# Seven natural tiles in 64x64 bursts, split loads and a new order in front of the steady phases

## The chip, the cores and the metric

The kernel runs on one core of a Trainium2 chip. TensorE (PE) multiplies, with its weight loads (PEld) beside it; VectorE (DVE), ScalarE (ACT) and GpSimd (POOL) work on tiles; POOL also issues the loads, SyncE (SP) the stores and the transposes by DMA. The metric is the device time of one execution in microseconds (us), the median of several.

## The reference, cut to what matters

```python
# q, k, v: (4, 8, 768, 64) float32
gamma = 1.0 - 2.0 ** (-5.0 - np.arange(H))
for t in range(S):
    state = gamma * state + k[t] v[t]^T            # per batch and head, 64 x 64
    y[:, :, t] = 1 / sqrt(64) * q[t] state
x = y.transpose(0, 2, 1, 3).reshape(3072, 512)
h = x @ w_in                                       # 512 x 2048
s = np.sin(alpha * h)
g = h + s * s / (alpha + 1e-09)
out = g @ w_out                                    # 2048 x 512
```

## The kernel before

**Tiles.** A tile is 128 positions of one batch with all 8 heads: 24 tiles, six to a batch (c = 0 to 5). `order` takes the four first tiles of the batches, e0 to e3, and then the others, batch by batch; `P` is the same list, so P[4] is the fifth tile, and P[4] to P[8] are batch 0, P[9] to P[13] batch 1. `groups` (L53) are e0 to e3 as group 0, and then pairs: P[4] and P[5] are group 1, P[6] and P[7] group 2, and so on.

**Attention of a tile.** q and k are transposed (qkT), on PE (`half_T`, `stage_T`) or by DMA from SP (`turn`, L258). The scores within the tile go to PSUM (tile pa), are masked by DVE into aT, and multiply v, which has been scaled by a decay (`scale_v`, L143; mostly on POOL). The running state adds what earlier tiles left. DVE multiplies the sum by a decay table qg into xT, the transposed input of the feed-forward. The state is carried on: in PSUM (ps) with a block-diagonal bf16 copy (s_bd) written by ACT for natural tiles, and in float32 (s_f, added up by DVE) with a bf16 copy (s_q, written by ACT, by POOL in the last batch) for wide ones.

**Natural and wide tiles.** A natural tile is loaded with 128 positions on the 128 partitions (`load_chunk`); its matmuls use half of PE's rows or half of its columns (`stage_A`, `stage_M`, `stage_S`, `keep_S`). A wide tile (`wide(j)`, j >= 8 and not a first tile: P[10] and after) is loaded by `load_seq`, one DMA to a head for a whole batch, with half of the heads on each half of the partitions; its matmuls use quarters of the array, 64 by 64, and come in one `burst`: `inter` (state times q) of the old tile, `scores` of the new one, `sums` (k times v), then a `nop` that waits until `inter` is through, and `mix` (scores times v). A burst hands back what is run later: `mask` and `exit` (py to xT), `keep` (to s_f) and `hand` (s_f to s_q).

**Feed-forward.** A `Slot` makes 128 or more rows of h for a group: matmuls with w_in into ph (L450), sin on ACT (L453), its square on ACT or DVE (L458, L460), and the last step into gT on DVE (`add`, L465). `ff_out` multiplies gT by w_out into po (L475), 16 matmuls to an output tile; `take` copies po out of PSUM and stores it. `fill(n)` and `F(ts, fs)` place such output pieces by hand.

**PSUM.** Eight banks: four of tag mm (ph, po, transposes), two as the pair pa, and one each of tags ps and ty (py of the bursts, ps, py of the natural tiles, and for a while the first two output tiles).

**Order.** The schedule is by hand: each engine runs its instructions as the program emits them. The front works on e0 to e2 with idle matmuls between. Group 0 runs 128 columns short at first (slots 0 to 3 for three tiles, then one 4-slot strip for e3), then slots 4 to 15 with output pieces between. Lines 668 to 719 are the seam to group 1: the last pieces of group 0, transposes, attention of P[4] and P[5], and 16 `fill` pieces between. From then on `phase(g, ...)` runs each group in eight double slots, with the output pieces of the group before it between and the attention of two later tiles at slots 1 and 5 (2 and 5 in phase 1), by `at` and `where`.

**Queues.** POOL issues all loads of q, k, v and the weights in program order, with `scale_v` and the decay tables between; w_in and w_out come in four pieces each. SP issues the transposes by DMA and the stores, in program order.

Of the kernel before, what the change touches and what calls it, by code (L numbers as in the profile page):

```python
# [16 lines left out]
def kernel(  # L17
# [15 lines left out]
    nc = tc.nc  # L33
# [35 lines left out]

    def chunk_of(t, j):  # L70
# [19 lines left out]
    def spot(h):  # L90

        return h // NP, (h % NP) ^ (h // NP)

    def load_seq(bt, names="qkv"):
# [3 lines left out]
        if "q" in names:  # L98
# [3 lines left out]
        for name, src in (("q", q), ("k", k), ("v", v)):  # L102
            if name not in names:
                continue
            for h in range(H):
                b, at = spot(h)
                r = slice(64 * b, 64 * b + 64)
                o = tv[r, :, at, :] if name == "v" else tqk[r, :, "qk".index(name), at, :]
                nc.gpsimd.dma_start(out=o, in_=src[bt, h, cs[0] * C:, :].rearrange("(f i) d -> i f d", i=64))  # L109
# [8 lines left out]
    def load_w_in(i):  # L118
        nc.gpsimd.dma_start(out=w_in[:, :, i * fw:(i + 1) * fw], in_=w_in_v[:, :, i * fw:(i + 1) * fw])

    def load_w_out(i):
        nc.gpsimd.dma_start(out=w_out[:, i * fo:(i + 1) * fo, :], in_=w_out_v[:, i * fo:(i + 1) * fo, :])
# [25 lines left out]
    load_w_in(0)  # L148
# [5 lines left out]
    load_w_out(0)  # L154
# [38 lines left out]
    def later_tables():  # L193
        for b in range(2):
            for p in range(NP):
                nc.vector.memset(lgq[64 * b:64 * b + 64, p:p + 1], lng[NP * b + (p ^ b)])
# [23 lines left out]
    s_bd = [big.tile([128, NP, 128], BF16, name=f"s_bd{i}") for i in range(2)]  # L220
# [9 lines left out]
    def half_T(j, i, eng, tag="mm"):  # L230
# [3 lines left out]
        pt = psum.tile([128, NP, 128], BF16, name="pt", tag=tag, bufs=4 if tag == "mm" else 1)  # L234
# [8 lines left out]
    def stage_T(j, eng=None, tag="ty"):  # L243
        pt = psum.tile([128, 2 * NP, 128], BF16, name="pt", tag=tag, bufs=4 if tag == "mm" else 1)
        st["qkT", j] = work.tile([128, 2 * NP, 128], BF16, name="qkT", tag="qkT", bufs=6)
        for i in range(2):
            for p in range(NP):
                nc.tensor.transpose(pt[:, i * NP + p, :],
                                    raw["qk"[i], j][:, 2 * p:2 * p + 2, :].rearrange("p h d -> p (h d)"), ident)
# [24 lines left out]
    def stage_S(j):  # L274
        c = j % NCH
        if c == 0:
            st["ps"] = psum.tile([128, NP, D], F32, name="ps", tag="ps")
        ps = st["ps"]
        for p in range(NP):
            for e in range(2):  # L280
                nc.tensor.matmul(ps[64 * e:64 * e + 64, p, :], raw["k", j][:, 2 * p + e, :], raw["v", j][:, 2 * p + e, :],
                                 start=(c == 0 and p == 0), stop=True, skip_group_check=True)
        return ps

    def turned(to, ps, copy):

        copy(to[:, 0:2], ps[:, 0:2])
        for e in range(2):
            copy(to[64 * e:64 * e + 64, 2:4], ps[64 - 64 * e:128 - 64 * e, 2:4])

    def keep_S(j, ps):
        if wide(j + 1):
            turned(s_q[(j % NCH + 1) % 2], ps, nc.scalar.copy)
            return
        for e in range(2):
            r = slice(64 * e, 64 * e + 64)
            nc.scalar.copy(s_bd[(j % NCH + 1) % 2][r, :, r], ps[r, :, :])

    def stage_M(j, tag="ty"):
        c = j % NCH  # L300
# [3 lines left out]
        qkT, aT, vs = st["qkT", j], st["aT", j], raw["v", j]  # L304
        py = psum.tile([128, NP, 128], F32, name="py", tag=tag)
        if c > 0:
            for p in range(NP):
                for e in range(2):
                    r = slice(64 * e, 64 * e + 64)
                    nc.tensor.matmul(py[r, p, :], s_bd[c % 2][:, p, r], qkT[:, p, :],  # L310
                                     start=(p == 0), stop=True, skip_group_check=True)
        for p in range(NP):
            for e in range(2):
                nc.tensor.matmul(py[64 * e:64 * e + 64, p, :], vs[:, 2 * p + e, :], aT[:, e, p, :],
                                 start=(c == 0 and p == 0), stop=True, skip_group_check=True)
        x = xT[g][:, :, i * C:(i + 1) * C]
        if c == 0:
            nc.scalar.copy(x, py)
            return
        ps = stage_S(j) if c < NCH - 1 else None  # L320
        nc.vector.tensor_mul(x, py, qg[:, c])
        if ps is not None:
            keep_S(j, ps)
# [3 lines left out]
    def half(x):  # L327
        return slice(64 * x, 64 * x + 64)

    tiles4 = [(b, e) for b in range(2) for e in range(2)]  # L330

    def inter(j):

        qkT, s = st["qkT", j], s_q[j % NCH % 2]
        st["py", j] = [psum.tile([128, 512], F32, name=f"py{b}", tag=tag) for b, tag in enumerate(("ps", "ty"))]
        for m in range(2):
            for b, e in tiles4:
                last = nc.tensor.matmul(st["py", j][b][half(e ^ b), m * 128:(m + 1) * 128].rearrange("p (f i) -> p f i", f=2),  # L338
# [452 lines left out]
```

## Time and profile before

| what | us |
|---|---|
| median of 3 runs | 214.45 (213.43 to 217.16) |
| the profiled execution | 214.06 |
| its span, first to last instruction | 212.3 |
| PE busy | 203.6 |
| ACT busy | 158.7 |
| DVE busy | 153.3 |
| POOL busy, DMA issues included | 113.4 |
| first slot of group 0 starts | 15.94 |
| slot 4 starts | 24.18 |
| phase 1 starts | 49.99 |
| phase 2 starts | 62.52 |
| phase 3 starts | 78.99 |

The profiled execution is 1.8 us longer than its span. A busy PE is not PE at its peak. In the lists of waits a line gives who waited for whom, the total, how often and the longest; in the timeline, the start, the length, the engine, the line and the operation; in the table by stretch, the length and each engine's busy time in it. A line number is one of the kernel above.

### The profile page before, as it was taken

To read this page: it belongs to the slowest core of one execution; us is meant where nothing else is said; L and a number is where in the kernel's file an instruction comes from. 1 tells how busy PE (TensorE), PEld (TensorE's weight loads), DVE (VectorE), ACT (ScalarE), POOL (GpSimd) and SP (SyncE) were. 2 spreads that over 40 slices of the span, in tenths; PEclk is the share of its full clock that TensorE was granted. 3 is DMA by queue.
4 is the path that set the end of the run, shared out by engine and by line. 5 is a ranking of instruction groups with operands and counts; after the bars stand their busy time and mean duration, and the time that the engine had idled before them with its cause. 6 is when DMAs were issued, how large, how long until landed. Compare 5 with 4: busy or idle time off the path is not lost.

```text
span 212.3 us, 5584 instructions
## 1 busy us (share of the span) xinstructions
PE 203.6 (96%) x2242; PEld 131.0 (62%) x2242; DVE 153.3 (72%) x342; ACT 158.7 (75%) x335; POOL 113.4 (53%) x149
## 2 busy tenths in 40 slices
PE   7868989999999999999999999999999999999994
PEld 3534534457776766766666666667666666666653
DVE  5785599766887688688678787786887778666550
ACT  7677576877998887877867877876877777788821
POOL 8999877899889169899699821001121120000000
PEclk9999999999999999999999999999999999999999
DMA  9999999999999979999999994403713110110112
GB/s 131 149 172 197 206 206 175 138 194 184 136 149 83 211 78 155 173 91 156 155 163 133 164 146 102 99 12 90 78 39 88 56 45 7 49 49 3 49 49 99
DMA packets 100281, 24.74 MB, mean 117 GB/s; under 512 B 92816, under 2 KB 97312, under 8 KB 100256
## 3 DMA queue, kind: packets, MB, share of 16 engines
q0 software_dynamic: 77504, 13.38, 87.1%
q1 hardware_dynamic: 22608, 10.96, 26.0%
q8 instruction: 17, 0.28, 0.6%
q14 instruction: 8, 0.07, 0.1%
q10 hardware_dynamic: 144, 0.07, 0.1%
HBM read 27.27 MB, written 6.29 MB: 158 GB/s over the span
## 4 chain that ended last, share of the span: by engine, by line
PE 78%; DVE 7%; POOL 5%; DMA 4%; ACT 3%; issue 1%; DVEq 0%; POOLq 0%
PE po L475 36%; PE ph L450 34%; DMA w_out<-in_moe_w_out_dram 4%; DVE gT L465 4%; POOL qkr L84 2%; PE poh L500 2%; PE py L338 2%; DVE s L460 2%; ACT s L453 2%; PE py L381 1%; POOL vr L84 1%; DVE aT L271 1%; ACT s L458 1%; PE pa L349 1%; PE py L310 1%
## 5 line engine op out<-in xcount | busy, mean ns | idle before, releaser
L465 DVE SCALAR_TENSOR_TENSOR gT<-s,rec_alpha,ph 128x256 bf16<-128x256 f32 (+3 forms) x180 | 81.6, 495 | 34.1 <-ACT s L458 33.7
L453 ACT ACTIVATE s<-ph,alpha_sb 128x256 f32<-128x256 f32 (+3 forms) x180 | 78.5, 484 | 36.5 <-PE ph L450 36.4
L450 PE MATMUL ph<-xT,w_in 128*128 128x256 bf16 (+3 forms) x720 | 99.1, 280 | 2.4 <-DVE gT L465 1.2
L475 PE MATMUL po<-w_out,gT 128*128 128x512 bf16 x368 | 96.2, 380 | 0.8 <-DMA w_out<-in_moe_w_out_dram 0.7
L450 PEld LDWEIGHTS <-w_in 128*128 128x128 bf16 x720 | 69.7, 98 | 33.8 <-issue 2.6
L458 ACT ACTIVATE s<-s 128x512 f32<-128x512 f32 (+1 forms) x91 | 56.9, 625 | 2.9
L475 PEld LDWEIGHTS <-gT 128*128 128x128 bf16 x368 | 34.0, 98 | 27.2 <-DVE gT L465 1.8
L421 POOL CAST s_q<-s_f 128x256 bf16<-128x256 f32 x5 | 2.0, 396 | 44.3 <-DVE s_f L415 25.7
L143 POOL TENSOR_TENSOR v_seq<-v_seq,kgq 128x512 bf16<-128x512 bf16 x14 | 14.6, 1066 | 11.4 <-issue 6.4
L109 POOL DMA_DIRECT2D qk_seq<-in_q_dram x24 | 17.1, 755 | 2.4 <-DMA v_seq<-in_v_dram 2.2
L109 POOL DMA_DIRECT2D qk_seq<-in_k_dram x24 | 17.0, 738 | 1.7 <-DMA qk_seq<-in_q_dram 1.6
L109 POOL DMA_DIRECT2D v_seq<-in_v_dram x24 | 17.0, 743 | 0.8 <-DMA qk_seq<-in_k_dram 0.6
L487 DVE COPY o_sb<-po 128x512 f32<-128x512 f32 x19 | 13.1, 691 | 5.2 <-PE po L475 5.2
L358 DVE TENSOR_TENSOR aTw<-pa,maskq 128x768 bf16<-128x768 f32 x14 | 13.3, 951 | 0.0
L408 DVE TENSOR_TENSOR xT<-py,qg 128x256 bf16<-128x256 f32 x28 | 10.5, 415 | 0.0
L519 PE MATMUL spare<-warm 128*128 128x512 bf16 x25 | 9.1, 492 | 1.2 <-DVE warm L161 1.2
L143 POOL TENSOR_TENSOR vr<-vr,kg 128x512 bf16<-128x512 bf16 x9 | 9.5, 1056 | 1.0 <-DMA vr<-in_v_dram 0.8
L84 POOL DMA_DIRECT2D vr<-in_v_dram x10 | 9.3, 931 | 1.1 <-DMA w_out<-in_moe_w_out_dram 0.5
L271 DVE TENSOR_TENSOR aT<-pa,mask 128x1024 bf16<-128x1024 f32 x6 | 7.3, 1219 | 2.3 <-PE pa L267 2.3
L84 POOL DMA_DIRECT2D qkr<-in_q_dram x9 | 8.3, 923 | 1.1 <-DMA w_out<-in_moe_w_out_dram 0.6
L84 POOL DMA_DIRECT2D qkr<-in_k_dram x9 | 8.2, 909 | 1.0 <-DMA w_out<-in_moe_w_out_dram 0.5
L460 DVE TENSOR_TENSOR s<-s 128x512 f32<-128x512 f32 x6 | 6.5, 1080 | 2.6 <-ACT s L453 2.6
(94 smaller groups left out, 145.9 us busy)
## 6 DMA issues: line engine op xcount, KB each, us to landing
out_dram<-o_sb SPq DMA_DIRECT2D x23, 256.0 KB, 3.4
w_in<-in_moe_w_in_dram POOLq DMA_DIRECT2D x4, 512.0 KB, 13.0
w_out<-in_moe_w_out_dram POOLq DMA_DIRECT2D x4, 512.0 KB, 14.0
vr<-in_v_dram POOLq DMA_DIRECT2D x10, 128.0 KB, 6.1
qk_seq<-in_q_dram POOLq DMA_DIRECT2D x16, 80.0 KB, 6.7
qk_seq<-in_k_dram POOLq DMA_DIRECT2D x16, 80.0 KB, 5.0
v_seq<-in_v_dram POOLq DMA_DIRECT2D x16, 80.0 KB, 5.6
qkr<-in_q_dram POOLq DMA_DIRECT2D x9, 128.0 KB, 5.9
```

The costliest lines, as they stand in the source:

```text
L84: nc.gpsimd.dma_start(out=t, in_=chunk_of(src, j))
L109: nc.gpsimd.dma_start(out=o, in_=src[bt, h, cs[0] * C:, :].rearrange("(f i) d -> i f d", i=64))
L143: eng.tensor_mul(t, t, by[:, j % NCH, :, None].to_broadcast([128, H, D]))
L358: return {"mask": lambda: nc.vector.tensor_mul(aT, pa[:, :, 0:384].rearrange("p e (m t) -> p e m t", m=2), maskq[:, None, None, :].to_broa ...
L408: nc.vector.tensor_mul(x[:, 2 * b:2 * b + 2, :], py[b][:, 0:256].rearrange("p (m t) -> p m t", m=2), qg[:, c, 2 * b:2 * b + 2])
L450: nc.tensor.matmul(self.ph[:, m, :], w_in[:, i, f * 128:(f + 1) * 128], xT[g][:, i, self.lo:self.hi], start=(m == 0 and i == 0), stop=(i = ...
L453: nc.scalar.activation(out=self.s[:, m, :], in_=self.ph[:, m, :], func=ACTF.Sin, scale=alpha_sb[:, f:f + 1])
L458: nc.scalar.activation(out=self.s, in_=self.s, func=ACTF.Square)
L460: nc.vector.tensor_mul(self.s, self.s, self.s)
L465: nc.vector.scalar_tensor_tensor(gT[self.g][:, f, self.lo:self.hi], self.s[:, m, :], rec_alpha[:, f:f + 1], self.ph[:, m, :], op0=ALU.mult ...
L475: nc.tensor.matmul(po[g, ts], gT[g][:, f, ts * C:(ts + 1) * C], w_out[:, f, :], start=(f == 0), stop=(f == FF - 1))
L487: nc.vector.tensor_copy(o_sb, po[g, ts])
```

## The change

- Natural tiles P[4] to P[10] run in `burst` too, with 64 by 64 matmuls: `scores` gets a natural form, `round_of` does half of what is added up at a time (scores times v, and k times v) on the two halves of the positions, and the nop stands between the two rounds. `stage_S`, `keep_S`, `turned` and s_bd go; the state of batch 0's first tile is made by `first_state`.
- P[10] becomes natural; batch 1's `load_seq` is shorter by one tile.
- For P[8], P[9] and P[10] (`spread`) q and k are loaded with two DMAs each, heads in another order; `stage_T` turns one head at a time, 16 transposes for 8.
- Tags ps and ty become one tile of two banks, "two"; py of a burst is one tile, so `exit` and `keep` are one DVE instruction each. The first burst (`apart`) takes two banks of tag mm.
- w_in's pieces 0, 2 and 3 and w_out's piece 0 are loaded in halves. The tables and the loads behind them are reordered; `scale_v` of e0 to e3, and of P[9], is on DVE.
- The seam: the transposes of P[4] move into group 0's loop, its scores and the first burst ahead of the last pieces of output tiles 0 and 1; 12 `fill` pieces for 16. The copy of output tile 1 is on DVE.
- Phase 1: `keep`, `hand`, `exit` run ahead of the output pieces, the mask behind `add`; the output pieces end one slot earlier.

```diff
+    def head(b, m, e):
+        return 4 * m + 2 * e + (e ^ b)
+    heads = [(b, m, e) for m in range(2) for b in range(2) for e in range(2)]
+    def spread(j):
+        return j in order[8:11]
...
-                t = big.tile([128, H, D], BF16, name="vr", tag="vr", bufs=10)
+                t = big.tile([128, H, D], BF16, name="vr", tag="vr", bufs=11)
...
-            nc.gpsimd.dma_start(out=t, in_=chunk_of(src, j))
+            if name != "v" and spread(j):
+                for o in range(2):
+                    nc.gpsimd.dma_start(out=t[:, NP * o:NP * o + NP], in_=chunk_of(src, j)[:, o::2])
+            else:
+                nc.gpsimd.dma_start(out=t, in_=chunk_of(src, j))
...
     def wide(j):
-        return j >= NCH + 2 and j % NCH > 0
+        return j >= NCH + 3 and j % NCH > 0
...
-    load_w_in(0)
+    for h in range(2):
+        load_w_in(0, h)
...
-    load_w_out(0)
+    for h in range(2):
+        load_w_out(0, h)
...
+                for e in range(2):
+                    h = 4 * (p % 2) + 2 * e + p // 2
+                    nc.tensor.transpose(pt[half(e), i * NP + p, :], raw["qk"[i], j][:, h, :], ident)
...
+    def first_state(j):
+        ps = psum.tile([128, NP, D], F32, name="ps", tag="mm", bufs=4)
+        for b, m, e in heads:
+            h = head(b, m, e)
+            nc.tensor.matmul(ps[half(e), 2 * b + m, :], raw["k", j][:, h, :], raw["v", j][:, h, :],
+                             start=(b == 0 and m == 0), stop=True, skip_group_check=True)
+        nc.scalar.copy(s_q[1], ps)
+        nc.vector.tensor_copy(s_f, ps)
...
+        if not wide(j):
+            for p in range(NP):
+                for f, e in tiles4:
+                    nc.tensor.matmul(pa[half(f), e, 128 * p:128 * p + 128], qkT[half(e), NP + p, half(f)],
+                                     qkT[half(e), p, :], start=(p == 0), stop=True, skip_group_check=True)
...
+    def round_of(j, now, n):
+        py, aT, vs = st["py", j], st["aT", j], raw["v", j]
+        for b, m, e in heads:
+            f = e ^ n
+            last = nc.tensor.matmul(py[e][half(e ^ b), m * 128 + 64 * f:(m + 1) * 128], vs[half(f), head(b, m, e), :],
+                                    aT[half(f), e, 2 * (e ^ b) + m, 64 * f:],
+                                    start=False, stop=True, skip_group_check=True)
+        if now is not None:
+            ks, vs = raw["k", now], raw["v", now]
+            for b, m, e in heads:
+                f, h = b ^ n, head(b, m, e)
+                last = nc.tensor.matmul(py[b][half(e), 256 + 64 * m:320 + 64 * m],
+                                        ks[half(f), NP * (e ^ b) + 2 * m + e if spread(now) else h, :],
+                                        vs[half(f), h, :], start=False, stop=True, skip_group_check=True)
+        return last
...
+        last = inter(old, apart)
+        if not wide(old):
+            last = round_of(old, now, 0)
         more = scores(new) if new is not None else {}
...
+        behind(last)
+        if wide(old):
+            mix(old)
+            if now is not None and now is not old:
+                sums(now, py, 256)
+        else:
+            round_of(old, now, 1)
...
+    for j in (e0, e1):
+        scale_v(j, nc.vector)
+    for h in range(2):
+        load_w_in(2, h)
     decay_table(1)
+    decay_table(2)
     load_w_out(2)
-    decay_table(2)
-    load_w_in(3)
+    for h in range(2):
+        load_w_in(3, h)
     decay_table(3)
+    decay_table(4)
+    load_chunk(order[4], "qk")
     load_w_out(3)
-    decay_table(4)
-    load_chunk(order[4])
     decay_table(5)
-    for name, j in zip("qkv", (e0, e1, e2)):
-        load_chunk(order[5], name)
-        scale_v(j, nc.gpsimd)
+    load_chunk(order[4], "v")
+    for j in order[5:7]:
+        load_chunk(j)
...
-            run(fresh, "mask")
+            run(fresh, *(("keep", "hand", "exit") if g == 1 else ("mask",)))
...
-            while done < no * (n + 1) * nf // FF:
+            while done < min(no, no * (n + 1) * nf // (FF - 2 * (g == 1))):
...
             now.add()
+            if g == 1:
+                run(fresh, "mask")
...
-    F((0, 1, 2), (0,))
-    b.add()
+    F((0, 1, 2), (0, 1))
     c.add()
-    stage_M(e3, "pa")
+    stage_M(e3, psum.tile([128, 2, 512], F32, name="pye", tag="pa")[:, 0])
     d.add()
+    for j in (e2, e3):
+        scale_v(j, nc.vector)
...
+        if f == 9:
+            first_state(e0)
+        if f == 13:
+            stage_T(P[4], nc.vector, "pa")
     F((0, 1), (13,))
+    scale_v(P[4], nc.gpsimd)
+    m4 = scores(P[4])["mask"]
+    m4()
+    fill(3)
+    stage_T(P[5], nc.scalar, "mm")
+    fill(1)
     a.add()
+    scale_v(P[5], nc.vector)
+    fresh = burst(P[4], P[5], apart=True)
+    run(fresh, "keep", "hand", "mask", "exit")
     F((0, 1), (14,))
     F((0, 1), (15,))
...
     load_chunk(P[7])
     load_chunk(P[8], "qk")
     scale_v(P[6], nc.gpsimd)
+    load_chunk(P[9], "qk")
     load_chunk(P[8], "v")
+    scale_v(P[7], nc.gpsimd)
+    load_chunk(P[10], "qk")
+    load_chunk(P[9], "v")
+    scale_v(P[8], nc.gpsimd)
+    load_chunk(P[10], "v")
     load_seq(1, "q")
     load_seq(1, "k")
     load_seq(1, "v")
     scale_v(P[10], nc.gpsimd)
...
+    fill(2)
     stage_T(P[6], nc.scalar, "mm")
     fill(3)
+    run(burst(P[5], P[6]), "exit", "keep", "hand", "mask")
     fill(3)
...
+    at((2, 3), lambda: scale_v(P[9], nc.vector))
```

In the code as changed, `F` copies output tiles 0 and 1 out when the sixteenth piece is in, tile 0 by ACT and tile 1 by DVE.

More of the change, by code (lines that the diff above doesn't have):

```diff
@@ L272, in stage_A, with x_of @@
         st["aT", j] = aT
[L274 to L300, printed above, removed]
+    def first_state(j):
[6 more added lines that the diff above has]
+        nc.vector.tensor_copy(s_f, ps)
+    def x_of(j):
         g, i = place[j]
@@ L303, in stage_M @@
             xT[g] = work.tile([128, KS, sizes[g] * C], BF16, name="xT", tag="xT", bufs=3)
[L304 to L311, printed above, removed]
+        return xT[g][:, :, i * C:(i + 1) * C]
@@ L320, in stage_M, with inter @@
[L320 to L328, printed above, removed]
+                nc.tensor.matmul(py[half(e), p, :], vs[:, 2 * p + e, :], aT[:, e, p, :],
+                                 start=(p == 0), stop=True, skip_group_check=True)
+        nc.scalar.copy(x_of(j), py)
     tiles4 = [(b, e) for b in range(2) for e in range(2)]
-    def inter(j):
+    def inter(j, apart):
@@ L334, in inter @@
         qkT, s = st["qkT", j], s_q[j % NCH % 2]
[L335 to L338, printed above, removed]
-                                        s[half(e), 2 * b + m, :], qkT[half(e), m:m + 5:4, half(b)],
-                                        start=(m == 0), stop=True, skip_group_check=True)
+        if apart:
+            st["py", j] = [psum.tile([128, 512], F32, name=f"py{e}", tag="mm", bufs=4) for e in range(2)]
+        else:
+            py = psum.tile([128, 2, 512], F32, name="py", tag="two")
+            st["py", j] = [py[:, e] for e in range(2)]
+            st["pyw", j] = py
```

199 lines of the change are left out of this document (82 added, 117 removed).

## The prediction

> **What bounds the kernel now.** I read the page first, then busy time by stage, then the waits and the timeline at the seams.
>
> ```profile
> PE 203.6 (96%) x2242; PEld 131.0 (62%) x2242; DVE 153.3 (72%) x342; ACT 158.7 (75%) x335; POOL 113.4 (53%) x149
> ```
>
> ```profile
> 24.18:40.47 16.29, 15.44 (x72) 6.82 (x71) 14.89 (x21) 12.32 (x21) 12.64 (x14) 1.00 1.71 186
> 40.47:49.99 9.52, 9.29 (x126) 5.21 (x125) 5.80 (x8) 7.20 (x14) 9.52 (x12) 1.00 1.92 167
> 49.99:62.52 12.53, 12.17 (x148) 9.27 (x146) 9.88 (x18) 11.13 (x26) 11.22 (x17) 1.00 2.22 159
> 62.52:78.99 16.47, 16.47 (x168) 11.01 (x168) 11.91 (x25) 13.91 (x33) 10.12 (x14) 1.00 1.26 125
> 78.99:94.50 15.51, 15.51 (x209) 10.52 (x208) 12.46 (x30) 12.21 (x27) 14.89 (x21) 1.00 1.70 141
> ```
>
> Columns of the stretches: length, then busy PE, PEld, DVE, ACT, POOL, then clock, DMA, GB/s. From 62.52 on (phase 2) PE has no gap at the full clock, so nothing done earlier by DVE or ACT counts there. What can move lies before: the front up to 24.18, group 0 (DVE 14.89 of 16.29 busy, as full as PE), the seam 40.47 to 49.99 (every engine but POOL idles in turn), and phase 1, where ACT idles only at its start.
>
> ```profile
> PEld L450 <- DMA w_in<-in_moe_w_in_dram: 1.7, 1, 1.7
> ...
> DVE aT L271 <- PE pa L267: 2.3, 2, 1.3
> ```
>
> ```profile
> 53.58 0.41 PE L310 MATMUL py<-qkT,s_bd 128*64 128x128 bf16 x8
> ...
> 54.60 0.39 PE L475 MATMUL po<-w_out,gT 128*128 128x512 bf16 x1
> ...
> 81.69 0.31 PE L338 MATMUL py<-qkT,s_q 64*64 64x128 bf16 x8
> ...
> 81.83 0.23 PE L349 MATMUL pa<-qkT 64*64 64x128 bf16 x4
> ...
> 82.00 0.30 PE L368 MATMUL pa<-v_seq,qk_seq 64*64 64x64 bf16 x16
> ...
> 82.13 0.34 PE L381 MATMUL py<-aTw,v_seq 64*64 64x128 bf16 x16
> ...
> 82.41 0.39 PE L475 MATMUL po<-w_out,gT 128*128 128x512 bf16 x1
> ```
>
> ```profile
> L258 SPq DMA_TRANSPOSE qkT<-qkr x2: 1482/1780/2078, 49.6 to 52.6; - x2
> ...
> DMA to landing us min/median/max: 8.0/8.0/8.0
> ...
> DMA to landing us min/median/max: 3.0/6.4/8.8
> ```
>
> Of these three fences the first shows waits over the span and in the seam (total, times, longest). The second is the timeline (start, length): a natural tile's attention holds PE from 53.58 to 54.60 (1.02 us, 32 matmuls); the 64x64 burst takes 81.69 to 82.41 (0.72, 56 matmuls). The third: transposes by DMA land 8.0 us after issue for natural tiles, and 3.0 to 8.8 over the span.
>
> **The change, part by part.** The profiled execution took 214.06 us, its span 212.3 and 1.8 around it; it lies 0.4 under the median 214.45. I sum against 214.06.
>
> *Front (to 24.18).* Slots 0 and 1 need half of w_in's first piece. The whole lands at 15.9 (issued 7.65, 8.2 to landing). The piece before it landed at 12.6, so half lands near 14.3, and xT of the third tile is ready at 14.9 (ACT, 14.34 + 0.58). Slot 0 then starts 1.0 earlier. But slot 4 needs w_in's second piece, landing at 12.30 + 11.2 = 23.5, so its 24.18 cannot move by more than 0.66. Taken: -0.6; ends -0.66 and 0. The two scale_v at 15.7 and two before the 4-column slot (4 x 0.68 = 2.7 on DVE) lie in DVE's idle of 2.0 before 17.68 and 2.58 before 24.91; without that cover they would cost the excess. The memsets of s_bd that go (0.55) lie under the wait for the first load.
>
> *Group 0's loop (24.18 to 40.47).* Into it move the first state (8 matmuls, 0.11; ACT copy, 0.39; DVE copy, 0.28 to 0.55 by the 128x128 row once or twice) and the fifth tile's transposes (0.45 on PE by the same stage's 43.46 to 43.91; DVE copy 0.69). PE: +0.56. DVE: +1.1 against 1.4 idle, of which 0.7 lies at the stage's start. The first state's bank is one of the four of tag mm, free while slot 10 sits in the pa pair. w_out's last piece now lands after q and k of the fifth tile (0.96 each by the trace: 36.2 becomes 38.1, they 38.1 become 35.6): F(12) wants the one at 39.4, the transposes the other at 36.9, so both are covered, by 1.3 us each; later loads cost what exceeds that. Taken +0.56; ends +0.5 and +1.1.
>
> *Seam (40.47 to 49.99, 9.52).* After, by program order from t = end of F(13): scores 0.27; mask 1.22, last add 0.75, scale 0.68 on DVE (t+2.9); inter and first round wait that add's bank, second round ends t+3.25; keep 2 x 0.28, mask 1.22, exit 2 x 0.42 (t+5.9); the copy of output tile 1, new on DVE, 0.69 (t+6.6), frees the bank pair "two"; burst of the sixth tile 0.81 and its exit 0.69 (t+8.1). With latencies 8.3, so -1.2. PE alone needs 6.1 (12 pieces and 4 of F at 0.22, two times 8 transposes, bursts, scores): end -3.4; other end 0, all lost on the new wait for the bank pair. It leaves 14 output pieces for phase 1, not 10.
>
> *A natural burst.* 56 matmuls: inter 8 (0.14, from 81.69 to 81.83), scores 16 of 128 columns (the row's 0.17 for 8 + 8 of 64, by columns 0.23 to 0.27), two rounds with 16 of 64 to 128 columns and 16 sums (0.28 + 0.13). Sum 0.81 for 1.02. Ends: 0.72, the wide burst itself; 1.02, nothing won.
>
> *Phase 1 (12.53).* PE: two bursts -0.42, four more pieces +0.86. ACT: eight sin and square rows at 1.43 = 11.4, plus two hands at 0.39 where before two pairs of s_bd took 0.74 each, plus the copy of output tile 3 (0.57) now inside: 12.8, as before. The mask after the add takes 1.2 off the chain that the critical path shows (DVE gT, xT, aT, gT). DVE's busy rises to 12.3 (keep 0.42 each), so three engines are within 0.7 of one another. PE's own sum is +0.44; taken +0.3, for the shorter chain; ends -0.3 and +0.9.
> A rule speaks against the tiling here: the Trainium skill, TensorEngine Tiling (Array Packing), PSUM Bottleneck, says that tiling speeds the matmuls and not the emptying of PSUM, which may become the bound. In this stage the rows agree (ACT has no idle left between 51 and 62.5); by the rule the bursts' 0.42 is worth nothing there, by the PE row -0.42. The sum would be 213.5 by the rule and is 213.1 by the rows.
>
> *Phase 2 (16.47).* PE-bound. Its two bursts were 1.14 and 0.99 and become 0.81: phase 2 tends to phase 3's 15.51 with wide bursts, plus 2 x 0.09, or 15.70: -0.77. Ends -0.96 and -0.3. The eleventh tile, made natural, costs 0.81 for 0.72 in phase 3: +0.09.
>
> *Steady phases.* exit and keep become one DVE instruction each (0.69 for 2 x 0.42, about 0.42 for 2 x 0.28), on an engine 80% busy beside a full PE: 0. Were DVE to bind, it would be a gain of 0.3 per burst. The end is untouched: 0.
>
> *Loads.* POOL is full from 40 to 70. It loses four scale_v (1.06 each) and gains 13 DMAs (108 become 121): four weight halves, and for tiles 9 to 11 q and k in two pieces each and the eleventh's v. A half is priced like w_in's 512 runs, 0.80, against 0.92 whole. POOL keeps eight in flight (an issue waits until the eighth before it landed: 16.18 after 15.9), so early halves delay nothing while DMA is the limit. Later they do. P8's last half is issued about 45.2 where k was issued at 43.69, and lands 4.9 to 5.9 later, at 50.1 to 51.1; the transpose takes 8.0, so 58.1 to 59.1. Its scores are due at 57.9 (slot 5 at 56.6 to 57.5, inter and first round 0.35). Wait 0.2 to 1.2, or 0 if the transpose takes 6.4: taken +0.4. Behind it stand the other transposes on SP and output tile 3's store, with a free buffer. P11: its k came at 61.7 + 3.9 = 65.6; POOL adds 2.6 (P8, P9), 4.0 (P10) and 1.1 (a scale now ahead), so 73.3; a transpose of 4.6 to 8.8 ends at 77.9 to 82.1; due at 80.3. Taken +0.3; ends 0 and +1.8.
> The Trainium skill, DMA: Bandwidth & Descriptors, Anatomy of one DMA, puts a fixed 2.0 us on every software DMA; paid in a row, the 13 would add 26 us. The rows say otherwise: landings come 0.9 apart though each takes 4.5, so it is latency behind eight others. I keep POOL's issue time.
>
> Sum: -0.6 +0.56 -1.2 +0.3 +0.4 -0.77 +0.09 +0.3 = -0.9: **213.1 us**.
>
> **The rivals.**
> *Late transposes (slower).* Place: P8's, P9's and P11's turn on SP, behind POOL. Each us that P8's last half lands after 49.9 (57.9 - 8.0), or P11's k after 73.8 (80.3 - 6.5), goes straight onto PE. For it: 8.0 twice, POOL full, P11's loads 7.7 later. Against: transposes of 3.1 where POOL is quiet. With both at their late ends (+0.8 and +1.5 on the sum) 215.4. It decides from 0.9 of added wait; over 2% needs 5.6.
> *The seam runs at PE's pace (faster).* If DVE's chain overlaps, -3.4 in place of -1.2, and phase 1 takes none of the +0.3 and waits: 213.1 - 2.2 - 0.7 - 0.4 = 209.8. For it: PE idles there only in waits of 0.3 to 1.3 on DVE and ACT. Against: eight DVE instructions in a row, 6.6 us.
> *DVE binds group 0 (no gain).* Its +1.1 lands whole, and the seam gives half: 213.1 + 0.5 + 0.6 = 214.2. For it: 14.89 of 16.29. Against: its idle just before each of the last two adds.
>
> **How the numbers follow.** Forecast 0.45, DVE binds 0.2, late transposes 0.22 (a quarter of it beyond 218), seam at PE's pace 0.13. About 2% (4.3 us, 210.2 to 218.7) is what a measurement of this kernel can tell from no change. Of the fast case 0.09 lies below 210.2, of the late case 0.07 above 218.7: faster 0.09, same 0.84, slower 0.07. The forecast's own range is 211.5 to 214.5; with its rivals 210.2 to 216.8.
>
> **What would show it.** Slot 0 near 14.9 and slot 4 near 23.6; loop end near 40.4; phase 1 at 48.8 and phase 2 at 62.1; a natural burst of 0.8; phase 2 of 15.7. Wrong if scores of P8 or P11 wait for a transpose by over 2 us, if a natural burst takes over 1.0, or if the first burst waits for its banks past 43.5.

## The result, and the profile after

The changed kernel took 211.7 us, the median of four runs (211.14 to 212.23); the kernel before took 214.22 beside it. One of its four runs, 217.16, was a slow one and stays out of the ratio, which is 0.9912, its 95% interval 0.9885 to 0.9939: by it about 1.9 us faster (2.5 by the medians as they stand), and within the 2% that the chances called "same". The profiled execution took 212.17 us for 214.06 before, its span 210.3 for 212.3. The forecast was 213.1.

The totals of the page of the changed kernel (engine, busy time, share of the span, instructions):

```profile
PE 202.7 (96%) x2418; PEld 129.9 (62%) x2418; DVE 156.6 (74%) x326; ACT 154.9 (74%) x325; POOL 117.2 (56%) x157
```

PE has 176 more instructions and 0.9 us less busy time. DVE and ACT have changed places as the busier of the two. Where the time went is in the same table by stretch as before: the front's slots, group 0's loop, the seam, phases 1, 2 and 3 (length, then busy PE, PEld, DVE, ACT, POOL, then clock, DMA, GB/s).

```profile
14.73:22.36 7.63, 7.52 (x69) 4.40 (x69) 7.06 (x12) 5.12 (x11) 7.57 (x9) 1.00 1.42 199
22.36:40.15 17.79, 16.49 (x95) 7.18 (x93) 16.33 (x24) 12.70 (x22) 13.11 (x15) 1.00 1.72 186
40.15:48.41 8.26, 7.72 (x177) 4.38 (x177) 6.25 (x12) 3.64 (x5) 8.26 (x12) 1.00 1.96 162
48.41:61.05 12.64, 12.64 (x207) 9.47 (x207) 10.57 (x21) 10.97 (x25) 12.13 (x16) 1.00 2.00 156
61.05:76.87 15.82, 15.82 (x211) 10.78 (x209) 13.35 (x27) 13.35 (x30) 15.09 (x24) 1.00 1.56 152
76.87:92.50 15.63, 15.63 (x209) 10.64 (x208) 11.87 (x25) 12.18 (x27) 15.45 (x22) 1.00 2.08 146
```

| stage | before | after | difference | forecast |
|---|---|---|---|---|
| up to slot 4 | 24.18 | 22.36 | -1.82 | -0.6 |
| group 0's loop | 16.29 | 17.79 | +1.50 | +0.56 |
| seam | 9.52 | 8.26 | -1.26 | -1.2 |
| phase 1, P8's wait with it | 12.53 | 12.64 | +0.11 | +0.3 and +0.4 |
| phase 2 | 16.47 | 15.82 | -0.65 | -0.77 |
| from phase 3 to the end | 133.29 | 133.43 | +0.14 | +0.09 and +0.3 |
| sum | | | -1.98 | -0.9 |

So the forecast came near the time, but not by its terms: the front gave three times what was forecast and the loop took nearly three times, and the waits for late transposes, 0.7 us of the sum, are not there.

The seam ran as it was written down beforehand. These are DVE's instructions in it, from the timeline of the changed kernel (start, length, engine, line, operation, and in brackets the idle time before it with what ended it):

```profile
40.69 1.23 DVE L349 TENSOR_TENSOR aT<-pa,mask 128x1024 bf16<-128x1024 f32 x1 [0.39 <-PE pa L346]
41.83 0.74 DVE L496 SCALAR_TENSOR_TENSOR gT<-s,rec_alpha,ph 128x512 bf16<-128x512 f32 x1
42.48 0.68 DVE L156 TENSOR_TENSOR vr<-vr,kg 128x512 bf16<-128x512 bf16 x1
43.69 0.48 DVE L446 TENSOR_TENSOR s_f<-s_f,py 128x128 f32<-128x128 f32 x2 [0.53 <-PE py L402]
44.10 1.22 DVE L349 TENSOR_TENSOR aT<-pa,mask 128x1024 bf16<-128x1024 f32 x1
45.23 0.75 DVE L436 TENSOR_TENSOR xT<-py,qg 128x256 bf16<-128x256 f32 x2
45.89 0.68 DVE L518 COPY o_sb<-po 128x512 f32<-128x512 f32 x1
47.67 0.69 DVE L433 TENSOR_TENSOR xT<-py,qg 128x512 bf16<-128x512 f32 x1 [1.09 <-PE py L402]
```

Mask, add, scale, keep, mask, exit and the copy of output tile 1 follow each other with one gap, the 0.53 us for the first burst's second round, and the sixth tile's burst starts at 46.63, when that copy gives the banks free. DVE's chain sets the stage's length, as forecast; PE was idle for 0.54 us.

A natural burst lasts 0.86 us where the forecast had 0.81 and the kernel before 1.02. PE's timeline of the eighth tile's, in the changed kernel:

```profile
57.53 0.31 PE L336 MATMUL py<-qkT,s_q 64*64 64x128 bf16 x8
...
57.73 0.24 PE L402 MATMUL py<-vr,qkr 64*64 64x64 bf16 x6
57.80 0.23 PE L346 MATMUL pa<-qkT 64*64 64x128 bf16 x2
...
58.09 0.30 PE L395 MATMUL py<-aT,vr 64*64 64x64 bf16 x7
...
58.39 0.39 PE L506 MATMUL po<-w_out,gT 128*128 128x512 bf16 x1
```

From 57.53 to 58.39 nothing waits, the scores of P[8] at 57.80 included: its transpose by DMA, issued at 50.16, had landed at 57.04.

The loop is where time was lost. First DVE and then POOL in it, from the timeline of the changed kernel:

```profile
20.54 2.49 DVE L156 TENSOR_TENSOR vr<-vr,kg 128x512 bf16<-128x512 bf16 x2
23.08 1.40 DVE L491 TENSOR_TENSOR s<-s 128x512 f32<-128x512 f32 x1
...
26.21 1.89 DVE L491 TENSOR_TENSOR s<-s 128x512 f32<-128x512 f32 x1
...
29.46 0.68 DVE L491 TENSOR_TENSOR s<-s 128x512 f32<-128x512 f32 x1
```

```profile
21.05 2.88 POOL L229 TENSOR_TENSOR qg<-qg,step 128x512 f32<-128x512 f32 x2
...
26.47 1.08 POOL L229 TENSOR_TENSOR qg<-qg,step 128x512 f32<-128x512 f32 x1
```

The same square on DVE (line 491) takes 0.68 us alone, and 1.40 and 1.89 beside POOL's decay tables (line 229); the two scalings take 2.49 where two take 1.29 elsewhere. PE pays for it twice:

```profile
25.69 1.02 PE L481 MATMUL ph<-xT,w_in 128*128 128x512 bf16 x4 [0.58 <-DVE gT L496]
28.95 0.82 PE L506 MATMUL po<-w_out,gT 128*128 128x512 bf16 x3 [0.72 <-DVE gT L496]
...
30.99 0.32 PE L294 MATMUL ps<-vr,kb 128*64 128x64 bf16 x8
...
36.52 0.64 PE L264 MATMUL pt<-ident,qkr 128*64 128x128 bf16 x16
```

Idle time on PE in the loop went from 0.85 to 1.30, and busy time from 15.44 to 16.49; of the latter 0.96 is the first state (0.32) and the fifth tile's transposes (0.64). This profile is the longest of its kind here: from slot 4 to the fifth tile's scores (line 346) it takes 17.86, where the profiles of e3 to e7 below, which have the tables in the loop too, take 17.21 to 17.24 and pay for it once, with 0.56 to 0.77.

### The profile page after: what moved, and what is told of

It is laid out like the page before. It is cut to its first block, busy times and chain, and to the rows that moved or that the text cites. A ratio compares the mean times of both kernels' runs of the same rounds, so it can differ in the third digit from the quotient of the medians.

```text
span 210.3 us, 5890 instructions
## 1 busy us (share of the span) xinstructions
PE 202.7 (96%) x2418; PEld 129.9 (62%) x2418; DVE 156.6 (74%) x326; ACT 154.9 (74%) x325; POOL 117.2 (56%) x157
## 4 chain that ended last, share of the span: by engine, by line
PE 84%; DVE 7%; POOL 2%; DMA 2%; ACT 1%; issue 1%; POOLq 0%; DVEq 0%; ACTq 0%
PE ph L481 37%; PE po L506 36%; PE py L336 2%; DMA qkr<-in_k_dram 2%; DVE gT L496 2%; PE poh L531 2%; DVE s L491 2%; PE py L386 1%; POOL qkr L100 1%; DVE aT L286 1%; DVE aT L349 1%; PE pa L346 1%; ACT s L484 1%; POOL vr L100 1%; PE py L395 1%
## 5 line engine op out<-in xcount | busy, mean ns | idle before, releaser
L156 POOL TENSOR_TENSOR v_seq<-v_seq,kgq 128x512 bf16<-128x512 bf16 x13 | 13.7, 1074 | 5.0 <-DMA v_seq<-in_v_dram 5.0
L433 DVE TENSOR_TENSOR xT<-py,qg 128x512 bf16<-128x512 f32 x19 | 13.0, 685 | 1.1 <-PE py L402 1.1
L361 DVE TENSOR_TENSOR aTw<-pa,maskq 128x768 bf16<-128x768 f32 x13 | 12.4, 953 | 0.0
L100 POOL DMA_DIRECT2D vr<-in_v_dram x11 | 10.3, 932 | 0.7 <-DMA w_in<-in_moe_w_in_dram 0.5
L349 DVE TENSOR_TENSOR aT<-pa,mask 128x1024 bf16<-128x1024 f32 x7 | 8.5, 1219 | 0.4 <-PE pa L346 0.4
L452 ACT CAST s_q<-s_f 128x256 bf16<-128x256 f32 x14 | 5.5, 391 | 3.6 <-DVE s_f L446 3.2
L156 POOL TENSOR_TENSOR vr<-vr,kg 128x512 bf16<-128x512 bf16 x5 | 5.5, 1105 | 3.1 <-DMA vr<-in_v_dram 3.1
L100 POOL DMA_DIRECT2D qkr<-in_k_dram x7 | 6.2, 893 | 1.1 <-DMA w_out<-in_moe_w_out_dram 1.1
L336 PE MATMUL py<-qkT,s_q 64*64 64x128 bf16 x160 | 6.4, 228 | 0.4 <-DVE o_sb L518 0.3
```

What stands on the lines that cost most here:

```text
L156: eng.tensor_mul(t, t, by[:, j % NCH, :, None].to_broadcast([128, H, D]))
L336: last = nc.tensor.matmul(o, s[half(e), 2 * b + m, :], to, start=(m == 0), stop=True, skip_group_check=True)
L361: return {"mask": lambda: nc.vector.tensor_mul(aT, pa[:, :, 0:384].rearrange("p e (m t) -> p e m t", m=2), maskq[:, None, None, :].to_broa ...
L433: nc.vector.tensor_mul(o, st["pyw", old][:, :, 0:256].rearrange("p b (m t) -> p b m t", m=2), by)
```

## The experiments

The theory: the halves bring the first loads, and so the front, forward; the loop gives part of it back because DVE's squares and scalings are held up by POOL's multiplications; seam, phase order and 64x64 tiles give what they were priced at; transposes are not late. No run takes the 64x64 tiles or the new seam out by themselves, so what these two give is read from the table by stage and not tested. The rivals, by experiment: the loop is longer only through its added PE work; the time comes from the loads alone; the late transposes decide.

The start of slot 4 moves, though the loads ahead of it are the same: from 22.36 to 23.98 in the eight profiles of kernels that share the changed one's first loads, and with it the wait of line 312's weight load for the fourth tile's v (0.4 us in the changed kernel, 1.8 in e10). So a stretch is compared from slot 4 on, and medians beside it. Even that is not quite fair: a later slot 4 leaves less of the tables in the loop.

**e1_whole.** The changed kernel with the four weight pieces whole.

```diff
-    for h in range(2):
-        load_w_in(0, h)
+    load_w_in(0)
# the same for load_w_out(0), load_w_in(2), load_w_in(3)
```

> The changed kernel with all four weight pieces loaded whole again. Theory A (the halves are what brings the front forward, and the front's gain reaches the end): slot 0 back near 15.9, slot 4 near 23.5 to 24.2 instead of 22.36, and the time 1.0 to 1.6 us over the changed kernel. Rival B (group 0's loop is set by DVE, which gives the front's gain back whatever the front does): slot 4 late by as much, but the loop shorter than its 17.79, and the time within 0.4 us of the changed kernel.

Median 212.53, ratio 0.9944 (0.9923 to 0.9965). Slot 4 is back at 24.14, but phase 1 starts at 48.91, only 0.50 after the changed kernel's 48.41: the stretch between is 24.77 long instead of 26.05. All six squares of the loop take 0.68 or 0.69 here, because POOL was through with the tables earlier against the loop: at 24.71, 0.57 after slot 4 began, where the changed kernel's last table ends 5.19 after it. So 1.8 us at the front was worth 0.5 at phase 1, and the missing 1.3 is in the loop. The time lies 0.83 over the changed kernel's by the medians, between the two expectations, and the intervals of the two ratios overlap.

**e2_before_halves.** The kernel before with the same four pieces in halves, nothing else.

```diff
-    load_w_in(0)
+    for h in range(2):
+        load_w_in(0, h)
# the same for load_w_out(0), load_w_in(2), load_w_in(3)
```

> The kernel before with the four weight pieces in halves and nothing else changed. Theory A: slot 4 near 22.5 and a time 1.0 to 1.6 us under before. Rival B: slot 4 earlier by 1 us or more, the loop longer than 16.29 by about as much, the time within 0.5 us of before.

Median 213.35, ratio 0.9987 (0.9964 to 1.0009). Slot 4 starts 0.60 earlier (23.58) and phase 1 by 0.62; at the median no difference can be measured. The halves alone do not make the 0.9%. One square of its loop, beside POOL's scaling from 31.90 to 32.95, is the longest in any of these loops:

```profile
31.39 2.56 DVE L464 TENSOR_TENSOR s<-s 128x512 f32<-128x512 f32 x1
```

**e3_decay_late.** In the changed kernel the last three decay tables later on POOL, behind loads.

```diff
-    decay_table(3)
-    decay_table(4)
...
-    decay_table(5)
...
     for j in order[5:7]:
         load_chunk(j)
+    decay_table(3)
+    decay_table(4)
...
+    decay_table(5)
     load_seq(1, "q")
```

> The changed kernel with POOL's decay tables 3 and 4 moved behind the loads of the seventh tile, where POOL waits for a landing, and table 5 ahead of batch 1's loads. Theory B (a multiplication on POOL slows DVE's instructions that read and write SBUF alone, and that is what makes the loop long): the two scale_v on DVE before the strip take 1.3 instead of 2.49, the squares there 0.7 instead of 1.40 and 1.89, the waits of PE for gT before slot 7 and before F(5) (0.58 and 0.72) shrink below 0.3, the loop ends 0.8 to 1.5 us earlier, and the time is 0.5 to 1.2 us under the changed kernel. Rival C (these instructions are long by themselves, or the loop is set by PE and the loads): lengths as before, the time within 0.3 us.

Median 212.19, ratio 0.9919 (0.9895 to 0.9943): no different from the changed kernel. DVE's squares in its loop, and POOL's tables where they are now:

```profile
23.41 0.69 DVE L491 TENSOR_TENSOR s<-s 128x512 f32<-128x512 f32 x1 [1.30 <-ACT s L484]
25.83 0.68 DVE L491 TENSOR_TENSOR s<-s 128x512 f32<-128x512 f32 x1
...
36.54 1.98 DVE L491 TENSOR_TENSOR s<-s 128x512 f32<-128x512 f32 x1
```

```profile
35.89 2.06 POOL L229 TENSOR_TENSOR qg<-qg,step 128x512 f32<-128x512 f32 x2
```

The two squares that had been slow take 0.69 and 0.68, and PE's two waits are gone; but the tables landed on another square, now 1.98, for which PE waited 0.77 at 39.36. The slow square goes where the tables go. That is the mechanism shown, and an edit that only moves the loss.

**e4_exit_last.** In the changed kernel the first burst's `exit` behind output pieces 14 and 15, so that the copy of output tile 1 comes ahead of it on DVE.

```diff
-    run(fresh, "keep", "hand", "mask", "exit")
+    run(fresh, "keep", "hand", "mask")
     F((0, 1), (14,))
     F((0, 1), (15,))
+    run(fresh, "exit")
```

> The changed kernel with the first burst's exit moved behind the copy of output tile 1 on DVE, so that the copy that frees the bank pair does not wait for it. Theory (the seam is set by DVE's chain through that bank pair): the second burst starts near 46.0 instead of 46.63, phase 1 near 47.9 instead of 48.41, the time 0.4 to 0.6 us under the changed kernel. Rival (the seam is set by ACT's copy of the sixth tile's transposes, which ends at 46.67, or by PE): 0 to 0.2 us.

Median 212.47, ratio 0.9936 (0.9907 to 0.9966), which does not part it from the changed kernel. The copy starts at 45.50 instead of 45.89, the second burst at 46.52 instead of 46.63: PE's own pieces end just before, and they are the next limit. Some 0.2 us is all that there was: from the fifth tile's scores to phase 1 it takes 7.97 instead of 8.19.

**e5_p8_late.** P[8]'s q and k loaded behind P[9]'s.

```diff
-    load_chunk(P[8], "qk")
+    load_chunk(P[9], "qk")
     scale_v(P[6], nc.gpsimd)
-    load_chunk(P[9], "qk")
+    load_chunk(P[8], "qk")
```

> The changed kernel with the loads of q and k of the ninth and the tenth tile exchanged, so that the ninth's land about 4 us later (near 52 instead of 47.6) and its transpose starts near 52.2 instead of 50.16. Theory (the transpose has about 0.8 us of slack in the changed kernel: it lands at 57.04, and its scores run at 57.8; every us beyond goes straight onto PE): it lands at 58.5 to 59.5, PE waits 0.7 to 1.7 us in the burst of phase 1's sixth slot, and phase 2 starts that much later. Rival (the transpose is short when nothing else of its kind stands beside it, or PE's wait is filled later): it lands by 57.8, and phase 2 starts within 0.2 us of 61.05.

Median 212.47, ratio 0.9933 (0.9898 to 0.9969). P[8]'s last half landed at 55.17 instead of 47.57, and PE then waited for the transpose, by its timeline:

```profile
59.42 0.42 PE L346 MATMUL pa<-qkT 64*64 64x128 bf16 x16 [0.43 <-DMA qkT<-qkr]
```

Phase 1 is 13.17 long instead of 12.64. So the rival's wait exists, at its place, but 7.6 us of delay cost half a microsecond: the changed kernel had 0.8 in hand (57.04 to 57.80), and the transpose, issued as soon as the half had landed, took 4.07 us from issue to landing, not the 6.88 it took in the changed kernel nor the 8.0 of the natural ones before. The transposes of this run between 48 and 80 us take 4.0 to 8.6; what sets the length was not found.

**e6_phase1_order.** Phase 1 in the old order: mask ahead, output pieces spread as before.

```diff
-            run(fresh, *(("keep", "hand", "exit") if g == 1 else ("mask",)))
+            run(fresh, "mask")
-            while done < min(no, no * (n + 1) * nf // (FF - 2 * (g == 1))):
+            while done < no * (n + 1) * nf // FF:
...
-            if g == 1:
-                run(fresh, "mask")
```

> The changed kernel with phase 1 in the order of before: the mask right behind the burst, exit, keep and hand at the next slot, the output pieces spread over all eight slots. Theory (phase 1 is now full on PE, 12.64 of 12.64, because the mask of 1.22 us no longer stands on DVE ahead of the last step of the slot): waits of PE for gT come back, and phase 1 takes 13.0 to 14.0 us. Rival (ACT's 11 us or PE's own work set phase 1 in either order): 12.4 to 12.8.

Median 213.95, ratio 0.9981 (0.9947 to 1.0015): without this order the kernel is no faster than the one before. Phases 1 and 2 by stretch, and from PE's timeline the two instructions that waited:

```profile
48.20:61.60 13.40, 12.45 (x204) 9.43 (x206) 10.91 (x21) 11.06 (x24) 13.35 (x19) 1.00 1.89 160
61.60:78.31 16.71, 15.81 (x206) 10.79 (x208) 13.15 (x27) 13.46 (x30) 16.39 (x25) 1.00 1.70 147
```

```profile
61.60 1.03 PE L481 MATMUL ph<-xT,w_in 128*128 128x256 bf16 x8 [0.64 <-DVE xT L433]
64.24 1.03 PE L481 MATMUL ph<-xT,w_in 128*128 128x256 bf16 x8 [0.51 <-ACT o_sb L520]
```

Phase 1 is 0.76 longer than the changed kernel's and phase 2 by 0.89, the largest effect of one part found here. 1.15 of the 1.65 are the two waits: phase 2's first slot waits for the exit into xT, and a slot soon after for the copy of an output tile, both late out of phase 1. The other 0.5 is put down to no wait (0.6 of the idle time left is missing records). The forecast had all this as "taken +0.3, for the shorter chain".

**e7_half_scores.** The natural tiles' scores in 8 matmuls on half of PE's rows and all its columns instead of 16 on quarters.

```diff
-                for f, e in tiles4:
-                    nc.tensor.matmul(pa[half(f), e, 128 * p:128 * p + 128], qkT[half(e), NP + p, half(f)],
+                for e in range(2):
+                    nc.tensor.matmul(pa[:, e, 128 * p:128 * p + 128], qkT[half(e), NP + p, :],
```

> The changed kernel with the scores of the natural tiles made by 8 matmuls on half the array, as before, in place of 16 on a quarter, so that a natural burst has 48 matmuls and changes the array's division twice more. Theory (changing the division costs more than the matmuls saved, since the columns passed are the same): a natural burst of 0.95 to 1.10 us instead of 0.86, phases 1 and 2 longer by 0.2 to 0.4 each. Rival (the number of matmuls decides): 0.75 to 0.85, phases shorter by 0.1.

Median 213.04, ratio 0.9973 (0.9947 to 1.0). Eight matmuls fewer, and the burst is longer. The eighth tile's, without its first two lines:

```profile
57.83 0.28 PE L402 MATMUL py<-vr,qkr 64*64 64x64 bf16 x8
58.03 0.40 PE L346 MATMUL pa<-qkT 64*128 64x128 bf16 x8
58.36 0.30 PE L395 MATMUL py<-aT,vr 64*64 64x64 bf16 x7
...
58.89 0.38 PE L506 MATMUL po<-w_out,gT 128*128 128x512 bf16 x1 [0.16 <-issue]
```

The mark that can be compared is the next piece of h (line 481): it comes 1.47 us after the burst's start (57.63 to 59.10) where it comes 1.30 after in the changed kernel (57.53 to 58.83). The 0.16 of idle time in the last line above is no wait: the order of the pieces has two matmuls there and the trace shows one, as some records are missing. So the burst is 0.17 longer, and the rows say where: the scores start 0.20 after the first sums began, not 0.07, and the second round 0.33 after the scores, not 0.29. Phases 1 and 2, with two bursts each, grow by 0.31 and 0.40 (12.95, 16.22). Half as many matmuls lose, and they lose it at the two places where the array's division now changes; that the change itself is the cause is not shown apart. The Trainium skill, TensorEngine Tiling (Array Packing), Key Properties, says that changing the tiling mode, and not just the tile, drains TensorE; the 0.17 us for two changes agrees with it.

**e8_tables_in_seam.** The changed kernel with the three tables later, at 46.08 in the seam and at 50.96 and 58.80 in phase 1, where DVE has no squares, and e4's edit.

```diff
-    decay_table(3)
-    decay_table(4)
...
-    decay_table(5)
...
     scale_v(P[6], nc.gpsimd)
+    decay_table(3)
     load_chunk(P[9], "qk")
     load_chunk(P[8], "v")
+    decay_table(4)
...
+    decay_table(5)
     load_seq(1, "q")
# and the exit behind pieces 14 and 15, as in e4_exit_last
```

> The changed kernel with decay tables 3 and 4 moved among the loads of the ninth and tenth tile, where DVE runs nothing that reads and writes SBUF alone, table 5 ahead of batch 1's loads, and the first burst's exit behind the copy of output tile 1. Theory (with the POOL multiplications gone from group 0's loop, nothing on DVE there is slow, also not the square of slot 13 that the first try hit): all squares of the loop 0.7, slot 4 to slot 15 in 14.4 instead of 16.04, phase 1 at 47.2 to 47.8, the time 0.6 to 1.2 us under the changed kernel. Rival (the loads set the seam: k of the sixth tile lands at 40 to 40.6, before which its transposes can't start): phase 1 near 48.0, 0.4 us or less.

Median 211.13 (210.56 to 211.8), ratio 0.9859 (0.9789 to 0.9929), the lowest of all. The squares of its loop, and below them, in the seam, an exit into xT beside the table that POOL multiplies from 46.08 to 47.18:

```profile
23.63 0.69 DVE L491 TENSOR_TENSOR s<-s 128x512 f32<-128x512 f32 x1 [1.81 <-ACT s L484]
26.05 0.69 DVE L491 TENSOR_TENSOR s<-s 128x512 f32<-128x512 f32 x1
28.10 0.68 DVE L491 TENSOR_TENSOR s<-s 128x512 f32<-128x512 f32 x1
...
46.39 0.69 DVE L433 TENSOR_TENSOR xT<-py,qg 128x512 bf16<-128x512 f32 x1 [0.81 <-PE py L402]
```

No square is slow, and the exit, which reads py from PSUM and only qg from SBUF, is not slowed by the table beside it. The Trainium skill, SBUF — State Buffer, Who interferes with whom, says that a VectorE instruction with two SBUF inputs contends with a GpSimd instruction that reads SBUF, that the one that starts first holds the shared pair of ports for its whole length, and that an instruction with at most one SBUF input, outside the 2-port modes, does not contend. On who contends the rows agree: squares (two SBUF inputs) stretch to as much as 2.56, masks, adds and exits (one input in PSUM) keep 1.22, 0.74 and 0.69. On who waits they do not settle it. The stretched squares of the kernel before and of the changed one end 0.55 to 0.57 after POOL's multiplication does, also the one at 26.21, which by the record starts 0.26 ahead of POOL's; but spans on POOL are rough. The 2.56 of e2 ends 1.0 after POOL's scaling and stays unexplained. From slot 4 to phase 1 e8 takes 24.23 instead of 26.05.

**e9_tables_whole and e10_tables_only.** e8 with the four weight pieces whole, and e8 without e4's edit. Their diffs are those of e1 and e4, the latter backwards.

> Three decay tables in the seam and the state's exit behind the last pieces, as in e8_tables_in_seam (span 209.1), but with w_in's pieces 0, 2, 3 and w_out's piece 0 whole again. Theory (halves bring the first loads forward by 1.8 us at slot 4, and with the multiplications out of group 0's loop that gain reaches phase 1): slot 4 at 24.1 instead of 22.9, loop 14.9 as in e8, phase 1 at 48.3, span 210.3, so 1.2 above e8. Rival (the loop's end is set by something that doesn't come earlier with the halves, as e1_whole's loop of 14.8 looked): phase 1 at 47.1 to 47.5 and span 209.1 to 209.5, as e8 within the jitter of the early loads.

> Tables in the seam as in e8_tables_in_seam, but the state's exit again ahead of the last two pieces of output tiles 0 and 1. Theory (e8's gain of 1.2 us is nearly all from the tables, the exit's place is worth 0.2): span 209.3 to 209.5, phase 1 at 47.3 to 47.6. Rival (the exit's place counts only once the loop is not held up by POOL, 0.5 or more): span 209.7 to 210.0, phase 1 at 47.7.

e9: median 212.61, ratio 0.9946 (0.9921 to 0.9971). e10: 211.54 (211.0 to 212.11), ratio 0.9903 (0.9875 to 0.9931). The stretch from slot 4 to phase 1 in the traces of e8, e9 and e10 (same columns as above):

```profile
22.90:47.13 24.23, 23.52 (x267) 11.58 (x271) 20.06 (x34) 16.24 (x27) 16.43 (x20) 1.00 1.81 178
```

```profile
24.39:48.81 24.42, 23.69 (x267) 11.48 (x270) 20.14 (x34) 16.24 (x27) 15.40 (x19) 1.00 1.76 181
```

```profile
23.88:48.34 24.46, 23.50 (x267) 11.63 (x271) 20.01 (x34) 16.24 (x27) 16.66 (x20) 1.00 1.76 172
```

e10's stretch is 0.23 longer than e8's: that is e4's edit. But its profile has slot 4 at 23.88, 0.98 later than e8's, with the same first loads, so its phase 1 (48.34) and span (210.3) met neither of the two numbers expected; the stage agrees with the theory, the totals cannot tell.

e9 closes the case of the front. The start of phase 1 (and of slot 4) in four profiles:

| | halves | whole |
|---|---|---|
| tables in the loop (changed kernel, e1) | 48.41 (22.36) | 48.91 (24.14) |
| tables in the seam (e8, e9) | 47.13 (22.90) | 48.81 (24.39) |

With the tables out of the way, 1.49 us at slot 4 is 1.68 at phase 1; with the tables in the loop, 1.78 is 0.50. The other profiles say the same: e10, 0.51 ahead of e9 at slot 4, is 0.47 ahead at phase 1, and e4 to e7, 0.2 to 1.5 ahead of e1 at slot 4, start phase 1 between 0.7 earlier and 0.5 later. The medians have the same order: 211.70 and 212.53, 211.13 and 212.61. That e8 is faster than the changed kernel rests on the stage, 1.6 to 1.8 us shorter in two traces than in the changed kernel's, and 0.8 to 1.5 shorter than in those of e4 to e7, which have the tables in the loop too (25.21 to 25.70). The medians (211.13 and 211.70, with ranges that overlap) do not prove it, nor does e10's.

## Why the prediction came out as it did

*Front, -0.6 for -1.82.* The step that failed: "slot 4 needs w_in's second piece, landing at 12.30 + 11.2 = 23.5, so its 24.18 cannot move by more than 0.66". That landing was taken as fixed. It moved: issued at 13.68 behind the halves, the piece landed at 21.89, and the changed kernel's trace has no wait for it in the front. The loads by the profile (KB each, median us from issue to landing), before and then after, for loads issued from 6 to 15 us:

```profile
w_in<-in_moe_w_in_dram POOLq DMA_DIRECT2D x3, 512.0 KB, 11.2
```

```profile
w_in<-in_moe_w_in_dram POOLq DMA_DIRECT2D x2, 256.0 KB, 5.5
w_in<-in_moe_w_in_dram POOLq DMA_DIRECT2D x1, 512.0 KB, 8.2
```

From 10 to 12 us the queue moved 166 GB/s instead of 146. Both figures spread: of the nine profiles with halves seven have 160 to 178 there and two (e2, e5) 144 and 145, the three with whole pieces 144 to 151. With whole pieces the second piece landed at 23.5 each time (before, e1, e9), with halves at 21.9 to 23.9 in the changed kernel and e2 to e7. So the halves bring it forward in most runs, and by less than here; why it spreads stays open. The changed kernel's profile was also an early one: over the eight profiles with its first loads slot 4 lies at 23.05 on the average, 1.2 ahead of the three with whole pieces (24.24). So against the 0.66 that was called the most, 1.2 is the figure that stands. Slot 0 at 14.9 was right (14.73).

*Loop, +0.56 for +1.50.* Two terms were mis-sized. PE's added work was priced at 0.11 and 0.45 and measured 0.32 and 0.64; the profile before had a row for the first of them, the same first state in 0.32 (line 281, at 44.05), and the transposes by single heads are 16 instructions, not 8. The rest, 0.45, is PE waiting for DVE. The rival "DVE binds group 0" came true in part, though not by its reason. DVE did get the 1.1 us more to do, in two copies of 0.42 and 0.69, and was busy 16.33; but e8 has the same copies, no wait of PE in the loop, and 16.26 from slot 4 to the fifth tile's scores where the changed kernel takes 17.86. What held PE up was DVE's instructions stretched by POOL, some 1.9 us in two squares and 1.2 in two scalings around the loop's start. The profile before had shown it. DVE's squares there, and one of POOL's scalings:

```profile
24.91 1.41 DVE L460 TENSOR_TENSOR s<-s 128x512 f32<-128x512 f32 x1 [2.58 <-ACT s L453]
...
30.26 1.17 DVE L460 TENSOR_TENSOR s<-s 128x512 f32<-128x512 f32 x1
...
37.96 0.69 DVE L460 TENSOR_TENSOR s<-s 128x512 f32<-128x512 f32 x1
```

```profile
29.82 1.05 POOL L143 TENSOR_TENSOR vr<-vr,kg 128x512 bf16<-128x512 bf16 x1
```

The six took 1.41, 0.85, 1.17, 1.19 and 1.17 beside POOL's tables and scalings, and 0.69 alone. The working read DVE's 14.89 of 16.29 as a load that it had to carry; 2.3 of it was waiting for POOL. The front's and the loop's errors hang together: an early slot 4 leaves more of the tables in the loop. Their sum, -0.32, is near the forecast's -0.04, so that the total came out near is in part luck.

*Seam, -1.2 for -1.26.* Right, by its own chain: the copy was forecast to end 6.6 us after the stage's start and ended 6.42 after, the exit of the sixth tile's burst 8.1 and 8.21. e4 shows that the next limit, PE's pieces, is 0.1 us behind, and PE was busy 7.72, not the 6.1 of the working, so the rival "seam at PE's pace" could not have given its 2.2.

*Natural bursts and phases 1 and 2.* 0.86 for 0.81; phase 2 -0.65 for -0.77. In phase 1 PE's busy time rose by 0.47, as its sum of 0.44 said, and its 0.36 of idle time went, so the phase grew by 0.11 only. The working had ACT at 12.8 and DVE at 12.3 there; they were busy 10.97 and 10.57 of 12.64 (ACT's row before, 11.13, was already below that sum). Phase 1 has no idle PE, so the rule on PSUM that was weighed there (bursts worth nothing because ACT empties it) did not bind in this order. In the old order (e6) PE waits 0.64 at the phase's end and 0.51 in the next: the rest of the change is worth nothing measurable without the order. Whether the order is worth anything without the tiling was not run.

*Transposes, +0.4 and +0.3 for 0.* P[8]'s last half was forecast to be issued at 45.2 and to land at 50.1 to 51.1; it was issued at 44.22 and landed at 47.57, in 3.35 us rather than 4.9 to 5.9. P[11]'s k landed at 70.24, not 73.3, and its transpose, from 70.30 to 74.55, was done 5.3 us before its scores ran at 79.83; even the next tile's (72.27 to 77.53) was done by then. The step that failed is POOL's queue taken as full: added issues were put in a row behind the old ones, each with its full time, and the half loads landed sooner too. The late rival's mechanism is real (e5) at about a tenth of its price.

## What to carry to other kernels

Before a busy engine is called the bound, compare the lengths of one instruction along its timeline: a square of 0.68 that is 1.2 in places is not all work: here the rest was contention, and it went where the neighbour went. When one load is split, the landings behind it must be worked out again; a landing read from the old trace is no bound. A gain at the front counts only as far as the stage behind it can take it: 1.8 us was worth 0.5 until the tables were moved. One profile's start can be a microsecond from the next one's, so a gain there is judged over several.

## What the runs showed of the hardware that was not expected

- Halving early weight pieces brought forward the piece behind them too, but not evenly: w_in's second piece landed at 21.9 to 23.9 in seven profiles with halves and at 23.5 in three without, and from 10 to 12 us the queue moved 144 to 178 GB/s with halves, 144 to 151 without. Why it spreads stays open.
- DVE's squares on SBUF of 128x512 f32 took 0.68 alone and up to 2.56 beside POOL's multiplications (most of them ended 0.55 to 0.57 us after POOL's), whereas instructions with one input in PSUM were not slowed.
- A transpose by DMA of one natural tile's q and k took 4.1, 5.5 and 8.5 us from issue to landing, with the same code, in e5 alone.
- Eight matmuls fewer, in another division of the array, made a burst 0.17 us longer (e7).
